# Attention and two expert layers on one core: routing columns and low parts moved from GpSimd to VectorE

## The chip, the cores and the metric

The kernel runs on one core of a Trainium2 chip. The metric is device microseconds (us) of one launch, lower is better. The core has five engines that work through instruction lists of their own in program order: TensorE (PE, with its weight loads PEld), VectorE (DVE), ScalarE (ACT), GpSimd (POOL) and SyncE (SP, which here only issues transfers). They wait for each other through semaphores.

## The reference

Chunked attention makes a matrix x of 2304 tokens by 512; a first expert layer sends each token to one of eight experts (top-1, with a capacity); a second layer weighs all eight experts with a matrix P that is normalized by rows and columns eight times.

```python
scores = scale * np.matmul(q_c, k_c.transpose(0, 1, 2, 4, 3))     # chunks of 64, B=4, H=8, S=576, D=64
attn = np.exp(scores - max); attn = attn / (attn.sum(-1) + 1e-09)
x = np.matmul(attn, v_c)                                          # then (B*S, H*D) = (2304, 512)
logits = x @ w_gate;  expert_idx = np.argmax(logits, axis=1)      # first layer, E=8, F=1024
# token i gets place counts[e] at its expert while counts[e] < capacity, and weight gate_w[i]
h = np.maximum(einsum('ecd,edf->ecf', disp, w1), 0.0);  y = einsum('ecf,efd->ecd', h, w2)
out[i] = gate_w[i] * y[expert_idx[i], pos[i]]                     # if kept
# second layer: P = exp(x @ w_gate2 - max), 8 times: rows / sum, columns / sum, * N/E
out += P[:, e:e+1] * (np.maximum(x @ w1[e], 0.0) @ w2[e])         # for all e
```

## The kernel before, in words

The kernel has three stages one behind the other: attention with routing (to about 150 us), the first expert layer (L641 to L853) and the second (L861 to L1194). The change lies in the first.

**Attention is a software pipeline written out by hand.** Its 18 tiles of 128 tokens go through 14 small steps (`st_tr` to `st_logits`). The loop at L596 runs n from 0 to 23 (called step n here), and in step n the table `order` (L593) issues each function for tile n minus its lag. So within step n an engine's instructions stand in this order: VectorE normalizes tile n-4 (`st_x1`, L390 to L393), makes the scale of tile n-5 (`st_scale`, L90 to L93), the low part of tile n-6 (`st_lo`, L416), and the row maximum and difference of tile n-2 (`st_max`, L361 and L363). ScalarE takes the exponential of tile n-3 (`st_exp`, L375), the high part of tile n-5 (`st_hi`, L412), the sum of squares of tile n-4 (`st_norm`, L401), a copy (L428), and four copies of transposed q or k (`st_tr`, L343, L346). The `manual_schedule` mode keeps that order; nothing is moved by a scheduler. GpSimd issues the store of each finished row of x (L418).

**Routing** (`route`, L442) is done for groups of three tiles. Its small VectorE steps are strewn between the pipeline's (`todo_r`): `second` of the five groups inside the loop falls on steps 9, 12, 15, 18 and 21. `r_row` (L516, VectorE) and `r_col` (L522, GpSimd) make two one-hot matrices whose product (`r_tab`, L527) fills the table `gidx` of tokens by expert and place. The sixth group comes after the loop (L626). The gathers of the first expert's tokens (L656, GpSimd) wait for `gidx` and for every store to `xs_d`, the last of which (`r_out`, L556) carries the tokens' weights.

**Expert 0's weights** are loaded and split beside this, by a plan of step numbers (L582): `w_stat` (L157, ScalarE) sums squares, `w_scale` adds them over the partitions (for expert 0 by GpSimd's `partition_all_reduce`, L176), `w_scale2` makes a power of two of it, and `w_split` makes a high and a low fp16 part of each quarter of a matrix. What is planned for step n is issued behind all else of step n. The quarters of matrix a are split at steps 10, 13, 8 and 15, those of b at 15, 14, 16 and 13, each in three instructions, VectorE, ScalarE, GpSimd (form 1):

```python
nc.vector.tensor_scalar(out=m.st[...], in0=m.st[...], scalar1=m.s, ...)          # L217
nc.scalar.copy(out=m.hi[...], in_=m.st[...])                                     # L218
nc.gpsimd.tensor_tensor(out=m.lo[...], in0=m.st[...], in1=m.hi[...], op=subtract) # L219
```

Before the loop VectorE converts the capacity (L573) and splits the second layer's gate (`gate_split`, L109), whose largest value goes through GpSimd's `partition_all_reduce` (L114).

## Time and profile before

| what | us |
|---|---|
| median of 3 runs | 1871.57 (1870.57 to 1871.91) |
| the profiled execution's own time | 1866.62 |
| its span, first to last instruction | 1864.9 |
| busy: PE / DVE / ACT / POOL | 1781.0 / 1016.5 / 721.4 / 483.1 |
| attention: GpSimd starts the first gather at | 146.32 |
| first expert layer: first matmul at | 152.87 |

The span is the part of the time in which instructions ran; 1.72 us of the profiled execution lie outside it. Busy shares over the whole span say little about the change, since it touches only the first 150 us; there the engines have to be read stretch by stretch.

### The profile page before, as it was taken

The numbers are of one execution on the slowest core, as the hardware profiler recorded it, in microseconds if no ns is written. First come the engines' busy times: TensorE is split into PE (matmuls) and PEld (weight loads), VectorE is DVE, ScalarE is ACT, GpSimd is POOL, SyncE is SP. The second block draws the span as 40 slices with busy tenths as digits, with TensorE's granted clock in tenths as the row PEclk, the third lists the DMA queues.
The fourth block names the chain that finished last, engine by engine and source line by source line (L and its number), as shares of the span: only waits on it lengthen the run. The fifth ranks groups of instructions, "written<-read, shape, count | busy, mean of one in ns | idle before, by whom it ended". The sixth has DMA issues, their size and how long they took to land.

```text
span 1864.9 us, 27396 instructions
## 1 busy us (share of the span) xinstructions
PE 1781.0 (96%) x10751; PEld 1011.4 (54%) x10751; DVE 1016.5 (55%) x1977; ACT 721.4 (39%) x1310; POOL 483.1 (26%) x498
## 2 busy tenths in 40 slices
PE   7877999888998999999999999999999999999998
PEld 5765666655454555555545555555555555555553
DVE  4896657756467734654464445355534653464432
ACT  7955556644334333441233323233322431242210
POOL 2255335541103300411031123012301321042221
PEclk9978999999999999999999999999999999999999
DMA  9746565844241203130221112112112120212200
GB/s 231 200 160 200 151 209 162 222 116 131 83 138 62 75 30 105 60 105 22 84 97 68 60 54 96 60 60 105 46 59 104 61 105 1 105 59 71 82 35 34
DMA packets 135118, 182.11 MB, mean 98 GB/s; under 512 B 62240, under 2 KB 80752, under 8 KB 134960
## 3 DMA queue, kind: packets, MB, share of 16 engines
q1 hardware_dynamic: 127968, 162.22, 28.1%
q0 software_dynamic: 5360, 17.24, 2.7%
q8 instruction: 98, 1.61, 0.4%
q14 instruction: 60, 0.49, 0.1%
q10 hardware_dynamic: 1632, 0.56, 0.1%
HBM read 149.21 MB, written 23.56 MB: 93 GB/s over the span
## 4 chain that ended last, share of the span: by engine, by line
PE 69%; DVE 4%; ACT 3%; issue 1%; POOL 1%; DMA 0%; POOLq 0%; DVEq 0%
PE p_m L1107 39%; PE p_m L1045 29%; DVE c L1051 1%; ACT eh L1061 1%; DVE el L1062 1%; ACT wsq L157 1%; POOL w L1080 1%; PE p_m L934 0%; ACT m L1070 0%; ACT m L1090 0%; PE p_l L166 0%; DVE w L222 0%; DVE u L1051 0%; ACT w L221 0%; DMA out_dram<-acc,rk 0%
## 5 line engine op out<-in xcount | busy, mean ns | idle before, releaser
L1107 PE MATMUL p_m<-w,eh 128*128 128x512 f16 x2304 | 686.2, 379 | 3.6 <-ACT eh L1061 3.6
L1045 PE MATMUL p_m<-x,w 128*128 128x384 f16 x4032 | 662.4, 326 | 1.7 <-DVE c L1051 1.3
L1045 PEld LDWEIGHTS <-w 128*128 128x128 f16 x4032 | 394.2, 98 | 263.0 <-issue 2.3
L1107 PE MATMUL p_m<-w,el 128*128 128x512 f16 x1152 | 437.1, 379 | 0.0
L1107 PEld LDWEIGHTS <-eh 128*128 128x128 f16 x2304 | 225.4, 98 | 270.7 <-ACT eh L1061 5.4
L1080 POOL TENSOR_TENSOR w<-u,m 128x384 f32<-128x384 f32 x96 | 96.6, 1006 | 970.5 <-DVE u L1051 911.3
L1061 ACT ACTIVATE eh<-c 128x384 f16<-128x384 f32 x384 | 190.3, 518 | 402.2 <-DVE c L1051 402.2
L1181 DVE SCALAR_TENSOR_TENSOR acc<-p_m,cf,acc 128x512 f32<-128x512 f32 x126 | 94.6, 750 | 383.3 <-PE p_m L1107 377.1
L1062 DVE SCALAR_TENSOR_TENSOR el<-c,eh 128x384 f16<-128x384 f32 x384 | 218.1, 569 | 126.6 <-ACT eh L1061 116.1
L1070 ACT COPY m<-p_m 128x384 f32<-128x384 f32 x96 | 44.7, 465 | 399.4 <-PE p_m L1045 399.4
L1107 PEld LDWEIGHTS <-el 128*128 128x128 f16 x1152 | 112.7, 98 | 137.1 <-DVE el L1062 1.8
L709 PEld LDWEIGHTS <-w 128*128 128x128 f16 x1152 | 106.2, 100 | 28.1 <-issue 11.2
L726 PE MATMUL p_y<-w,hh 128*128 128x512 f16 x352 | 106.6, 385 | 0.0
L709 PE MATMUL p_p<-xT,w 128*128 128x256 f16 x768 | 89.3, 278 | 9.6 <-DMA xT<-xg 3.8
L1085 POOL TENSOR_TENSOR c<-u,m 128x384 f32<-128x384 f32 x96 | 95.8, 998 | 1.5 <-DVE u L1051 1.5
L1051 DVE TENSOR_TENSOR u<-p_m,m 128x384 f32<-128x384 f32 x96 | 53.4, 556 | 59.6 <-PE p_m L1045 59.6
L1051 DVE TENSOR_TENSOR c<-p_m,w 128x384 f32<-128x384 f32 x96 | 53.5, 557 | 50.0 <-PE p_m L1045 32.2
L246 ACT ACTIVATE w<-wsum,wsa 128x1024 f16<-128x1024 f32 x32 | 36.6, 1145 | 87.1 <-POOL wsum L240 87.1
L222 DVE SCALAR_TENSOR_TENSOR w<-stb,wsb,w 128x1024 f16<-128x1024 f32 x46 | 65.3, 1431 | 6.2 <-ACT w L221 6.1
L1051 DVE TENSOR_TENSOR u<-p_m,u 128x384 f32<-128x384 f32 x96 | 53.5, 557 | 27.7 <-PE p_m L1045 25.6
L157 ACT ACTIVATE wsq<-sta 128x1024 bf16<-128x1024 f32 x64 | 67.6, 1056 | 0.9
L726 PE MATMUL p_y<-w,hl 128*128 128x512 f16 x176 | 67.7, 385 | 0.0
(232 smaller groups left out, 1664.8 us busy)
## 6 DMA issues: line engine op xcount, KB each, us to landing
x<-xt_d SPq DMA_DIRECT2D x147, 384.0 KB, 4.4
sta<-in_moe_w_dram SPq DMA_DIRECT2D x18, 1024.0 KB, 6.5
stb<-in_moe_w_dram SPq DMA_DIRECT2D x18, 1024.0 KB, 7.6
sta<-in_moe_w_dram SPq DMA_DIRECT2D x28, 512.0 KB, 8.7
stb<-in_moe_w_dram SPq DMA_DIRECT2D x28, 512.0 KB, 11.8
xt_d<-x SPq DMA_DIRECT2D x21, 384.0 KB, 3.5
x_d<-row SPq DMA_DIRECT2D x20, 256.0 KB, 4.1
vbd<-in_v_dram SPq DMA_DIRECT2D x72, 64.0 KB, 3.7
```

The lines of the kernel that those rows point to most:

```text
L157: nc.scalar.activation(out=sq, in_=src, func=AF.Square, accum_out=m.mx[:, h:h + 1])
L222: nc.vector.scalar_tensor_tensor(out=m.lo[:, sl, :], in0=m.st[:, sl, :], scalar=m.s, in1=m.hi[:, sl, :], op0=ALU.mult, op1=ALU.subtract)
L709: nc.tensor.matmul(p[:, f4, :], lhsT=w[:, kk, f * 128:(f + 1) * 128], rhs=xT[:, lo + kk, 0:W], start=(n == 0), stop=(n == 3 * KD - 1))
L726: nc.tensor.matmul(y, lhsT=h[:, kk, sl], rhs=w[:, kk, :], start=(n == 0), stop=(n == 3 * KF - 1))
L1045: nc.tensor.matmul(p, lhsT=wt[:, w, lw, kk, :], rhs=xt[:, lx, kk, :], start=(n == 0), stop=(n == 5))
L1051: nc.vector.tensor_tensor(out=c, in0=p, in1=t, op=ALU.add)
L1061: nc.scalar.activation(out=hh[:, sl], in_=src, func=AF.Relu)
L1062: nc.vector.scalar_tensor_tensor(out=hl[:, sl], in0=src, scalar=0.0, in1=hh[:, sl], op0=ALU.max, op1=ALU.subtract)
L1080: nc.gpsimd.tensor_tensor(out=Q["w"], in0=Q["u2"], in1=Q["m5"], op=ALU.add)
L1085: nc.gpsimd.tensor_tensor(out=Q["c22"], in0=Q["u3"], in1=Q["m5"], op=ALU.add)
L1107: nc.tensor.matmul(y, lhsT=h[:, t * 128:(t + 1) * 128], rhs=w[:, kk, :], start=(n == 0), stop=(n == 3 * KF - 1))
L1181: nc.vector.scalar_tensor_tensor(out=acc[:, j, :], in0=y, scalar=coefs[x][:, j:j + 1], in1=acc[:, j, :], op0=ALU.mult, op1=ALU.add)
```

## The change

It does six things. (1) `r_col` runs on VectorE. (2) The quarters of expert 0 are split in the form that the later experts use already: ScalarE makes the high part with the scale in it, and VectorE the low part (x times s, minus high) in one instruction; the last quarter of b moves from step 13 to step 17. (3) The sums over partitions of expert 0's weights are products with a matrix of ones on TensorE, and `w_scale` and `w_scale2` come a step later. (4) The capacity and the second gate are handled in steps 6 to 8, the gate's sum over partitions is a product too (a sum instead of a maximum; the exponent's offset goes from 4 to 11). (5) The sixth group's first steps and its counting product come ahead of step 23. (6) The rest of the sixth group is reordered: its weights are stored before its places are computed, and the counts come after its table.

```diff
--- before.py
+++ after.py
@@ -21,7 +21,6 @@
 EXP_MASK = 0x7F800000
-LW = 4
 LF = 10
 LM = 11
 LX = 5
@@ -107,19 +106,27 @@
     def gate_split(src, nm):
-        wgt = sm("gate", [128, KD, E])
+        wgt = const.tile([128, KD, E], F32, name="gate")
         nc.scalar.dma_start(out=wgt, in_=src.rearrange("(k p) e -> p k e", p=128))
-        gm, ga = sm("gm", [128, 1]), sm("ga", [128, 1])
-        nc.vector.tensor_reduce(out=gm, in_=wgt, axis=AX.XY, op=ALU.max, apply_absolute_value=True)
-        nc.gpsimd.partition_all_reduce(out_ap=ga, in_ap=gm, channels=128, reduce_op=bass.bass_isa.ReduceOp.max)
-        s, inv = pow2_of_max(ga, 1, LW, "gate")
         g = const.tile([128, KD, 2 * E], F16, name=nm)
-        nc.vector.tensor_scalar(out=g[:, :, 0:E], in0=wgt, scalar1=s, scalar2=None, op0=ALU.mult)
-        nc.vector.scalar_tensor_tensor(out=g[:, :, E:2 * E], in0=wgt, scalar=s, in1=g[:, :, 0:E],
-                                       op0=ALU.mult, op1=ALU.subtract)
         keep = const.tile([128, 1], F32, name=nm + "i")
-        nc.vector.tensor_copy(keep, inv)
-        return g, keep
+        t = {}
+
+        def largest():
+            t["m"] = sm("gm", [128, 1])
+            nc.vector.tensor_reduce(out=t["m"], in_=wgt, axis=AX.XY, op=ALU.max, apply_absolute_value=True)
+
+        def total():
+            t["s"] = over_partitions(t["m"], 296, 1)
+
+        def split():
+            s, inv = pow2_of_max(t["s"], 1, LM, "gate")
+            nc.vector.tensor_scalar(out=g[:, :, 0:E], in0=wgt, scalar1=s, scalar2=None, op0=ALU.mult)
+            nc.vector.scalar_tensor_tensor(out=g[:, :, E:2 * E], in0=wgt, scalar=s, in1=g[:, :, 0:E],
+                                           op0=ALU.mult, op1=ALU.subtract)
+            nc.vector.tensor_copy(keep, inv)
+
+        return g, keep, (largest, total, split)
     class Mat:
@@ -169,11 +176,7 @@
     def w_scale(x, nm):
         m = mats[x, nm]
         m.scaled = False
-        if x > 0:
-            m.am = over_partitions(m.mx, {"a": 288, "b": 292}[nm], 4)
-            return
-        m.am = smw("wam" + nm, [128, 4])
-        nc.gpsimd.partition_all_reduce(out_ap=m.am, in_ap=m.mx, channels=128, reduce_op=bass.bass_isa.ReduceOp.add)
+        m.am = over_partitions(m.mx, {"a": 288, "b": 292}[nm], 4)
     def w_scale2(x, nm):
         m = mats[x, nm]
@@ -205,17 +208,13 @@
         n = 2 * ((x - E) % 2) if x >= E else 2 * (nm == "b")
         m.hi, m.lo = (w_slot(x, n + i).rearrange("p (k n) -> p k n", n=m.n) for i in range(2))
-    def w_split(x, nm, j, nj, on_pool=0):
+    def w_split(x, nm, j, nj, on_pool=False):
         m = mats[x, nm]
         c = m.kk // nj
         sl = slice(j * c, (j + 1) * c)
-        if on_pool == 2:
+        if on_pool:
             nc.scalar.activation(out=m.hi[:, sl, :], in_=m.st[:, sl, :], func=AF.Copy, scale=m.s)
             nc.gpsimd.tensor_scalar(out=m.st[:, sl, :], in0=m.st[:, sl, :], scalar1=m.s, scalar2=None, op0=ALU.mult)
-            nc.gpsimd.tensor_tensor(out=m.lo[:, sl, :], in0=m.st[:, sl, :], in1=m.hi[:, sl, :], op=ALU.subtract)
-        elif on_pool == 1:
-            nc.vector.tensor_scalar(out=m.st[:, sl, :], in0=m.st[:, sl, :], scalar1=m.s, scalar2=None, op0=ALU.mult)
-            nc.scalar.copy(out=m.hi[:, sl, :], in_=m.st[:, sl, :])
             nc.gpsimd.tensor_tensor(out=m.lo[:, sl, :], in0=m.st[:, sl, :], in1=m.hi[:, sl, :], op=ALU.subtract)
         else:
             nc.scalar.activation(out=m.hi[:, sl, :], in_=m.st[:, sl, :], func=AF.Copy, scale=m.s)
@@ -519,7 +518,7 @@
             def r_col(j):
                 if j == 0:
                     t["cols"] = at.tile([128, G, E * NT], F16, tag="cols", name="cols")
-                nc.gpsimd.tensor_scalar(out=t["cols"][:, j, :], in0=iocf, scalar1=t["ci"][:, j:j + 1],
+                nc.vector.tensor_scalar(out=t["cols"][:, j, :], in0=iocf, scalar1=t["ci"][:, j:j + 1],
                                         scalar2=None, op0=ALU.is_equal)
             def r_tab():
@@ -570,25 +569,28 @@
             nc.gpsimd.memset(vbd[j][64:128, :, :, 129:130], 1.0)
         load_qk(1)
         nc.sync.dma_start(out=cap_i, in_=capacity.bitcast(I32).partition_broadcast(128))
-        nc.vector.tensor_copy(cap, cap_i[:, 0:1])
         nc.scalar.dma_start(out=g1, in_=w_gate.rearrange("(k p) e -> p k e", p=128))
-        g2, ig2 = gate_split(w2_gate, "g2")
+        sums["bank"] = p_tab
+        g2, ig2, g2_steps = gate_split(w2_gate, "g2")
         nc.vector.memset(ohsum[0], 0.0)
         todo = {}
         def plan(n, f):
             todo.setdefault(n, []).append(f)
-        for nm, ld, st, sc, sp in (("a", (2, 3), (3, 4, 5, 6), 6, (10, 13, 8, 15)), ("b", (9, 10), (11, 10, 12, 12), 12, (15, 14, 16, 13))):
+        plan(6, lambda: nc.vector.tensor_copy(cap, cap_i[:, 0:1]))
+        for n, f in zip((6, 7, 8), g2_steps):
+            plan(n, f)
+        for nm, ld, st, sc, sp in (("a", (2, 3), (3, 4, 5, 6), 6, (10, 13, 8, 15)), ("b", (9, 10), (11, 10, 12, 12), 12, (15, 14, 16, 17))):
             for h in range(2):
                 plan(ld[h], lambda nm=nm, h=h: w_load(0, nm, h))
                 plan(NT + 1, lambda nm=nm, h=h: w_load(1, nm, h))
             for h in range(4):
                 plan(st[h], lambda nm=nm, h=h: w_stat(0, nm, h, True))
-            plan(sc, lambda nm=nm: (w_scale(0, nm), w_alloc(0, nm)))
-            plan(sc + 1, lambda nm=nm: w_scale2(0, nm))
+            plan(sc + 1, lambda nm=nm: (w_scale(0, nm), w_alloc(0, nm)))
+            plan(sc + 2, lambda nm=nm: w_scale2(0, nm))
             for h in range(4):
-                plan(sp[h], lambda nm=nm, h=h: w_split(0, nm, h, 4, 1))
+                plan(sp[h], lambda nm=nm, h=h: w_split(0, nm, h, 4))
         order = ((st_x1, 4), (st_scale, 5), (st_exp, 3), (st_lo, 6), (st_scores, 2), (st_hi, 5), (st_norm, 4), (st_xtr, 4),
                  (st_max, 2), (st_xcopy, 4), (st_tr, 0), (st_pv, 3), (st_logits, 5), (st_dtr, 2))
@@ -599,6 +601,10 @@
             if 2 <= n < NT + 2:
                 load_v(n - 2)
             i = n - 6
+            if n == NT + 5:
+                (*first, tot1, tot2), mm, (gw, eps, rec, sel, pos, *second), tab, (kx, racc, rout) = route(NG - 1)
+                for r in first + mm:
+                    r()
             if i >= 0 and i % G == G - 1 and i < NT - G:
                 for m, part in zip((n, n + 1, n + 1, n + 3, n + 5), route(i // G)):
                     todo_r.setdefault(m, []).append(part)
@@ -623,8 +629,7 @@
             for part in todo_r[n]:
                 for r in part:
                     r()
-        (*first, tot1, tot2), mm, (gw, eps, rec, *second), tab, (kx, racc, rout) = route(NG - 1)
-        for r in first + mm + second + tab + [tot1, tot2, gw, eps, rec, racc, kx, rout]:
+        for r in [gw, eps, rec, sel, pos, kx, rout, *second, *tab, tot1, tot2, racc]:
             r()
         tot = sm("gtot", [128, 2, E, E], F16)
@@ -804,7 +809,7 @@
             if y < E:
                 for nm in "ab":
                     w_alloc(y, nm)
-                sp = [lambda h=h, nm=nm: w_split(y, nm, h, 4, 2 * (nm == "b" and h > 1)) for h, nm in
+                sp = [lambda h=h, nm=nm: w_split(y, nm, h, 4, nm == "b" and h > 1) for h, nm in
                       ((0, "a"), (2, "b"), (1, "a"), (2, "a"), (3, "b"), (3, "a"), (0, "b"), (1, "b"))]
                 sc = [lambda f=f, nm=nm: f(y, nm) for f in (w_scale, w_scale2) for nm in "ab"]
                 steps = sc + sp
```

**VectorE from the end of step 8 into step 9.** Here `sta` is the staged f32 matrix a of expert 0, `w` its fp16 part, `x1s` the scale of a tile. Before:

```order
L428 COPY xT<-p_t 128x512
L217 TENSOR_SCALAR sta_277<-sta_277,wsa 128x1024
L390 TENSOR_SCALAR rs<-p_x 128x8
L391 RECIPROCAL rs<-rs 128x8
L393 TENSOR_TENSOR x_768<-p_x,rs 128x512
L540 TENSOR_REDUCE ggw<-gex 128x3
L543 TENSOR_SCALAR ggw<-ggw 128x3
L90 TENSOR_SCALAR x1h<-ssq_696 128x1
L91 TENSOR_SCALAR x1s<-x1h 128x1
```

After the change:

```order
L187 TENSOR_REDUCE wmma<-p_tab 128x1
L89 TENSOR_SCALAR wh<-wmma 128x1
L90 TENSOR_SCALAR wsa<-wh 128x1
L92 TENSOR_SCALAR wia<-wh 128x1
L221 SCALAR_TENSOR_TENSOR w_1_630<-sta_262,wsa,w_0_629 128x1024
L389 TENSOR_SCALAR rs<-p_x 128x8
L390 RECIPROCAL rs<-rs 128x8
L392 TENSOR_TENSOR x_765<-p_x,rs 128x512
L539 TENSOR_REDUCE ggw<-gex 128x3
L542 TENSOR_SCALAR ggw<-ggw 128x3
L89 TENSOR_SCALAR x1h<-ssq_675 128x1
L90 TENSOR_SCALAR x1s<-x1h 128x1
```

The scaling of the quarter has become the subtraction that makes its low part; it reads `w`, which ScalarE writes at the end of its own step 8. The scale of the weights (L187 to L92), and ahead of that the gate's seven rows, stand before it, and step 9 with the next tile's normalization and scale stands behind it.

**VectorE before the first tile.** `gm` and `ga` are the gate's largest value by partition and over all of them. Before:

```order
L566 MEMSET kbd_157 128x2048
L573 CAST cap<-cap_i 128x1
L113 TENSOR_REDUCE gm<-gate 128x1
L79 TENSOR_SCALAR gatem<-ga 128x1
L80 TENSOR_SCALAR gatem<-gatem 128x1
L82 TENSOR_SCALAR gates<-gatem 128x1
L84 TENSOR_SCALAR gatei<-gatem 128x1
L117 TENSOR_SCALAR g_200<-gate,gates 128x4x8
L118 SCALAR_TENSOR_TENSOR g_200<-gate,gates,g_200 128x4x8
L121 COPY g2i<-gatei 128x1
L576 MEMSET ohsum_91 128x4
L361 TENSOR_REDUCE mx<-p_s 128x8
```

After the change:

```order
L565 MEMSET kbd_156 128x2048
L565 MEMSET kbd_157 128x2048
L575 MEMSET ohsum_91 128x4
L360 TENSOR_REDUCE mx<-p_s 128x8
L362 TENSOR_TENSOR d<-p_s,mx 128x512
```

The first row maximum now follows the clearing of `kbd` and of the counts.

**VectorE at the end of attention.** `gkr` is what the last store carries, `gidx` the table that the gathers read. Before, from the rows of the sixth group on:

```order
L516 TENSOR_SCALAR rows<-iorf,glo,tokf 128x128 x3
L480 TENSOR_REDUCE gohs<-goh_1982 128x8
L483 TENSOR_TENSOR ohsum_91<-ohsum_92,gohs 128x8
L540 TENSOR_REDUCE ggw<-gex 128x3
L543 TENSOR_SCALAR ggw<-ggw 128x3
L546 RECIPROCAL ggw<-ggw 128x3
L534 TENSOR_TENSOR gidx<-tacc,p_tab 128x144
L550 SCALAR_TENSOR_TENSOR gkx<-gpos,cap,ggw 128x3
L555 TENSOR_TENSOR gkr<-gkx,inv 128x24
```

After the change, from the places of the sixth group on:

```order
L491 TENSOR_REDUCE gpos<-gsel 128x3
L549 SCALAR_TENSOR_TENSOR gkx<-gpos,cap,ggw 128x3
L554 TENSOR_TENSOR gkr<-gkx,inv 128x24
L495 TENSOR_TENSOR gge<-gpos,iotf 128x54
L500 TENSOR_REDUCE ghi<-gge 128x3
L504 SCALAR_TENSOR_TENSOR glo<-ghi,gpos 128x3
L509 SCALAR_TENSOR_TENSOR gci<-gix,ghi 128x3
L515 TENSOR_SCALAR rows<-iorf,glo,tokf 128x128 x3
L521 TENSOR_SCALAR cols<-iocf,gci 128x144 x3
L479 TENSOR_REDUCE gohs<-goh_1960 128x8
L482 TENSOR_TENSOR ohsum_91<-ohsum_92,gohs 128x8
L533 TENSOR_TENSOR gidx<-tacc,p_tab 128x144
```

`gkr` now comes before L495, the three column rows (L521) stand on VectorE between the rows and the table, and the weights' sum and reciprocal (L540 to L546 before) have moved ahead of these rows. So have, ahead of the last low part, the sixth group's maximum to one-hot rows (L448 to L467 before).

## Rows read from the trace of the kernel before

**Rows 1.** Busy time by stretch: stretch, length, each engine (instructions), clock, DMA share, GB/s.

```profile
25.00:80.00 55.00, 49.09 (x536) 41.47 (x537) 41.42 (x132) 54.00 (x102) 12.96 (x16) 0.97 0.89 226
93.00:118.00 25.00, 16.07 (x148) 13.42 (x147) 24.48 (x43) 16.50 (x30) 18.67 (x14) 0.79 0.38 123
118.00:135.00 17.00, 15.41 (x164) 13.21 (x162) 16.11 (x68) 8.64 (x19) 4.80 (x8) 0.90 0.58 214
160.00:1864.90 1704.90, 1663.46 (x9600) 912.80 (x9597) 899.58 (x1619) 610.76 (x1111) 425.63 (x412) 0.99 0.28 89
```

**Rows 2.** Timeline, first tile: start us, us, engine, line, operation, what ended idle time.

```profile
11.75 1.98 PE L354 MATMUL p_s<-kbd,qT 128*64 128x128 f32 x16 [2.19 <-ACT qT L346]
16.11 0.15 DVE L79 TENSOR_SCALAR gatem<-ga 128x1 f32<-128x1 f32 x1 [4.12 <-POOL ga L114]
17.20 0.68 DVE L361 TENSOR_REDUCE mx<-p_s 128x8 f32<-128x512 f32 x1
```

**Rows 3.** Timeline and issues of SP, 16.6 to 21.8 us; TensorE's use of it.

```profile
16.63 5.19 SPq L329 DMA_DIRECT2D vbd<-in_v_dram  x4
vbd<-in_v_dram SPq DMA_DIRECT2D x4, 64.0 KB, 4.6
27.71 1.11 PE L384 MATMUL p_x<-vbd,eT 128*64 128x130 f32 x16
```

**Rows 4.** Timeline of VectorE, ScalarE and TensorE, steps 8 to 10.

```profile
51.01 0.74 DVE L217 TENSOR_SCALAR sta<-sta,wsa 128x1024 f32<-128x1024 f32 x1
51.67 0.16 DVE L390 TENSOR_SCALAR rs<-p_x 128x8 f32<-128x8 f32 x1
52.84 1.05 ACT L218 CAST w<-sta 128x1024 f16<-128x1024 f32 x1
53.16 0.15 DVE L91 TENSOR_SCALAR x1s<-x1h 128x1 int32<-128x1 int32 x1
54.41 0.71 ACT L412 ACTIVATE row<-x,x1s 128x512 f16<-128x512 f32 x1
55.00 0.86 DVE L516 TENSOR_SCALAR rows<-iorf,glo,tokf 128x128 f16<-128x128 f32 x3
56.49 0.69 DVE L363 TENSOR_TENSOR d<-p_s,mx 128x512 f32<-128x512 f32 x1
57.59 0.63 PE L370 MATMUL p_t<-ident,d 128*128 128x128 f32 x4
58.70 0.60 ACT L375 ACTIVATE eT<-p_t 128x512 f32<-128x512 f32 x1
```

**Rows 5.** Timeline of VectorE in the first expert layer: two low parts.

```profile
232.31 2.48 DVE L222 SCALAR_TENSOR_TENSOR w<-sta,wsa,w 128x1024 f16<-128x1024 f32 x2 [0.35 <-ACT w L221]
```

**Rows 6.** Timeline of VectorE at step 13 and of ScalarE at steps 14 and 15.

```profile
83.93 0.16 DVE L184 TENSOR_REDUCE wmmb<-wamb 128x1 f32<-128x4 f32 x1 [2.24 <-POOL wamb L176]
91.57 1.05 ACT L218 CAST w<-stb 128x1024 f16<-128x1024 f32 x1
93.13 0.71 ACT L412 ACTIVATE row<-x,x1s 128x512 f16<-128x512 f32 x1
```

**Rows 7.** Timeline of GpSimd and VectorE, steps 15 to 17.

```profile
93.18 2.16 POOL L219 TENSOR_TENSOR w<-sta,w 128x1024 f16<-128x1024 f32 x1 [7.66 <-ACT w L218]
93.26 2.62 DVE L416 SCALAR_TENSOR_TENSOR row<-x,x1s,row 128x512 f16<-128x512 f32 x1
113.08 1.78 DVE L458 SCALAR_TENSOR_TENSOR goh<-gd,ioef 128x24 f32<-128x24 f32 x1
```

**Rows 8.** Timeline of the end of attention.

```profile
139.43 0.18 DVE L487 TENSOR_TENSOR gsel<-goh,p_tab 128x24 f32<-128x24 f16 x1 [0.47 <-PE p_tab L476]
143.01 0.30 DVE L534 TENSOR_TENSOR gidx<-tacc,p_tab 128x144 int32<-128x144 f32 x1 [0.72 <-PE p_tab L527]
143.69 0.37 SPq L556 DMA_DIRECT2D xs_d<-gkr  x1
146.32 1.13 POOL L656 DMA_INDIRECT xg<-xs_d,gidx  x1 [3.68 <-DMA xs_d<-gkr]
```

## Prediction, made before the changed kernel ran

> **What bounds the kernel now.** I read the busy times by stretch first, then the timelines of attention, then the end of it. From 160 us on TensorE is busy 1663 of 1705 us [rows 1]; the change adds or removes nothing there, so whatever attention ends earlier or later is passed on one for one. Attention has no single bound. From 25 to 80 us ScalarE works 54.0 of 55.0 us: it is the bound, and each of its waits is lost. From 93 to 118 us VectorE works 24.48 of 25.0 us and ScalarE only 16.5. From 118 to 135 us VectorE still works 16.11 of 17.0 us [rows 1]. The reader should also see the fork that decides this case. At step 8 VectorE reaches its part of a split (L217) at 51.01 us, while ScalarE comes to its own at 52.84 us [rows 4]: before, VectorE went ahead and waited for nobody. Now its part reads what ScalarE wrote, and stands in front of all of step 9.
>
> **The head.** The first row maximum starts at 17.20 us behind the gate, which waited 4.12 us for GpSimd; its scores were done at 11.75 + 1.98 = 13.73 us [rows 2]. Without the gate it starts 0.1 us after them, at 13.85: at most 3.35 us earlier. Late next is a block of v. Its four transfers were issued until 16.63 + 5.19 = 21.82 us, with 4.6 us to landing, so about 26.4 us, and TensorE used it at 27.71 [rows 3]; that is 1.3 us of room. So the gain lies between 1.3 us, if ScalarE is soon short of that product, and 3.35, if it never is. I take 2.3, the middle, since no row is nearer to either end.
>
> **The splits.** One low part on VectorE takes 2.48 / 2 = 1.24 us [rows 5] instead of L217's 0.74 [rows 4]; ScalarE's part keeps its length within 0.1 us. Taken alone that is 8 x 0.5 = 4 us, but the wait is more. At step 8 ScalarE is done at 52.84 + 1.05 = 53.89 us. VectorE then needs 0.1 to start, 1.24 for the low part, and from L390 (51.67) to the end of L91 (53.16 + 0.15) 1.64 us for the next tile's normalization and scale. ScalarE's high part (L412) waits for that scale: it starts at 57.0 instead of 54.41 us, 2.6 us late [rows 4]. The gate's and the weights' scales at step 8 cost nothing, since VectorE would only wait longer without them.
>
> **The columns.** Three of them on VectorE are taken from L516: three rows of 128 elements took 0.86 us [rows 4], of which the next instruction overlaps about 0.1; with 144 elements that is between 0.77 and 0.97, and I take 0.81, as the setup of an instruction does not grow with its elements. In step 9, VectorE took from L91's end (53.31) to L363's end (57.18) 3.87 us; now 57.0 + 3.87 + 0.81 = 61.7, and with the 0.63 us of transposes and two hand-overs of 0.1 the exponential (L375) starts at 62.5 instead of 58.70 us [rows 4]. **Steps 8 and 9 together: +3.8.**
>
> **The other splits,** reckoned in the same way: +2.1 at step 10, where ScalarE has one more sum of squares to do while it waits; +0.8 at step 13, where VectorE already waits 2.24 us for the weights' sum [rows 6], a wait that ScalarE's part now replaces; +2.6 at step 14: ScalarE's part begins at 91.57, so the next high part begins 1.05 + 0.1 + 1.24 + 1.64 + 0.1 later, at 95.7 instead of 93.13 us [rows 6]. Four splits of one pattern, 9.3 us by the end of step 14.
>
> **What is given back.** While GpSimd subtracts (L219, 93.18 to 95.34), VectorE's L416 takes 2.62 us and ends just behind it. From it to L458 with 1.78 us [rows 7] six VectorE instructions are held so, 10.7 us together beyond what their lines take elsewhere. With GpSimd's subtractions and its columns gone these go. But at step 15 ScalarE's two parts again come last: the step is 3.1 us shorter, and step 16 begins 1.4 us sooner, together -4.5 in ScalarE's time. At steps 16 and 17 the pattern returns, with +2.3 and +2.0, the last for the split that was moved there. Then no split is left. The columns of steps 18 and 21 add 1.6, of which VectorE's 0.9 us of idle time [rows 1] takes a half to all: +0.7. **Steps 8 to 22: 3.8 + 2.1 + 0.8 + 2.6 - 4.5 + 2.3 + 2.0 + 0.7 = +9.8.**
>
> **The tail.** The gathers start at 146.32 us, 3.68 us idle behind the store of `gkr`, issued at 143.69: 2.63 us to be seen. The table's last row begins at 143.01 [rows 8]. After the change `gkr` is stored some 3.3 us earlier and is no longer last; the table is. Its chain loses the idle 0.47 and 0.72 us [rows 8], and gains 0.81 for the columns and 0.4 for the `gkr` rows ahead: it ends where it did, at 143.3, and the gathers start 0.15 later, 2.9 us earlier than before. If the columns take longer, 2.1. Expert 1's maxima stay on VectorE behind the table; I take them as hidden by the gathers, and if they are not, they cost at most the 0.4 us by which the counts now stand ahead of them. The load of expert 1's second matrix reuses the staging of the quarter that moved to step 17 and so starts later; it is needed by these maxima only, and costs nothing.
>
> **The sum.** -2.3 + 9.8 - 2.9 = **+4.6 us**. The profiled execution would go from 1866.62 to 1871.2 us; the median of the runs shown is 4.95 us above that execution, and I add the difference to the median: 1871.57 + 4.6 = 1876.2 us.
>
> **Rivals.** *VectorE is freed (faster).* If ScalarE's parts were done whenever VectorE reaches them, only VectorE's work would count: from 80 us on -10.7 (holds) - 2.2 (wait) + 6 x 0.5 + 3 x 0.81, about -7.5, with head and tail -12.7: 1858.9 us. For it speaks ScalarE's 8.5 idle us from 93 to 118 us; against it that it has one idle us from 25 to 80 [rows 1], where three of the seven split steps lie. It decides where VectorE's own step is longer than the 6 us that ScalarE needs to the end of its part. The Trainium skill stands on this side: GPSIMD Engine Reference (Engine selection) sends elementwise work to VectorE and calls GpSimd about twice as slow with two inputs. By that rule alone the eight subtractions are a plain gain; it says nothing of who waits, and the sum above goes by rows 4. The same table sends sums over partitions to GpSimd, against this change; here the row shows VectorE idle 2.24 us for one such sum, and by the rule that would have stayed, with the same result, since ScalarE's part ends later than both.
>
> *The waits shrink (no change).* ScalarE has slack behind 93 us. If it is ahead at steps 16 and 17, their 4.3 us go and the sum is +0.3: 1871.9 us. Against it: its high part at each of these steps still waits for VectorE's scale.
>
> *TensorE's clock falls (slower still).* From 93 to 118 us the granted clock is 0.79 on average, with TensorE busy 16 of 25 us [rows 1], against 0.97 at 49 of 55. If the new waits bring it to that for steps 8 to 17, each step's transposes and products on the path, about 2 us, grow by a quarter: 8 x 0.5, or +8.6 in all: 1880.2 us.
>
> **Chances.** The sum as forecast 0.44, the falling clock 0.13, the shrinking waits 0.27, VectorE freed 0.16. The likeliest case alone spans the bounds of head, columns and tail and a half us at four waits: +2 to +7, 1873.6 to 1878.6. The range of 1867.0 to 1881.0 takes in the two neighbours and the near side of the freed case, leaving out about 0.2. A measurement here tells about 0.2%, 3.7 us, from no change; of the forecast's 0.44 some 0.10 lie below that. So slower 0.34 + 0.13 = 0.47, same 0.10 + 0.27 = 0.37, faster 0.16.
>
> **What would show it.** Right: VectorE idle before its low parts (L221 in the new numbering) at steps 8, 10, 13, 14, 16 and 17, "behind ScalarE's w", with 1 to 5 us each; ScalarE idle about 2 to 3 us before the next high part; no held instruction of 1.5 us or more; the first row maximum near 13.9 us; GpSimd's first gather near 150.9 us with the table as its releaser. Wrong: if the low parts show no idle time ahead of them, or the first gather comes before 147 us; then the waits were not there and the time falls. If the first gather comes after 155 us, the columns or the clock cost more than I took.

## The result, and the profile after

The changed kernel is **slower**: 1885.63 us median of 4 runs (1883.96 to 1887.87) beside 1871.07 for the kernel before (4 runs, 1870.20 to 1871.91), a ratio of 1.0064 with a 95% interval of 1.0048 to 1.008. The forecast was 1876.2 us, in a range that ended at 1881.0: the direction was right and the loss some three times too small. The profiled execution took 1887.87 us, with a span of 1886.0.

Three marks carry what follows: the end of attention (the last low part of a row on VectorE), the first gather, and the first product of the first expert. From before to after they go from 137.56 to 150.45 us (+12.9), from 146.32 to 156.67 (+10.4), and from 152.87 to 163.19 (+10.3). From there to the end it is 1712.0 us before and 1722.8 after: another +10.8 us that the change should not have touched. The two profiled executions lie 21.3 us apart, the medians 14.6: the one before is 4.5 us below its median, the one after 2.2 above, so differences between these two traces come out somewhat large.

Busy time by stretch of the changed kernel (columns as in rows 1):

```profile
25.00:80.00 55.00, 46.84 (x483) 40.16 (x483) 38.02 (x132) 44.43 (x82) 4.04 (x7) 0.91 0.80 203
93.00:118.00 25.00, 21.99 (x178) 19.18 (x176) 17.84 (x53) 18.20 (x30) 2.41 (x4) 0.70 0.20 59
118.00:135.00 17.00, 12.02 (x110) 10.17 (x110) 14.10 (x53) 9.03 (x17) 1.24 (x3) 0.81 0.84 281
160.00:1886.00 1726.00, 1673.47 (x9670) 921.74 (x9670) 900.27 (x1633) 614.06 (x1115) 428.23 (x418) 0.99 0.28 89
```

Where one engine was full before [rows 1], none is now: from 25 to 80 us ScalarE works 44.4 of 55 us in place of 54.0, from 93 to 118 us VectorE 17.8 of 25 in place of 24.5 (part of that is the held time that is gone). Where neither is full, time goes into waiting for each other. The step 8 of rows 4 shows how, in the timeline of ScalarE and VectorE:

```profile
51.25 1.15 ACT L220 ACTIVATE w<-sta,wsa 128x1024 f16<-128x1024 f32 x1
52.43 1.28 DVE L221 SCALAR_TENSOR_TENSOR w<-sta,wsa,w 128x1024 f16<-128x1024 f32 x1 [1.33 <-ACT w L220]
55.13 0.15 DVE L90 TENSOR_SCALAR x1s<-x1h 128x1 int32<-128x1 int32 x1
55.32 0.72 ACT L411 ACTIVATE row<-x,x1s 128x512 f16<-128x512 f32 x1 [2.30 <-DVE x1s L90]
```

VectorE waits 1.33 us for ScalarE's high part, does its low part and step 9's normalization, and only then makes the scale that ScalarE has been waiting for, 2.30 us. The view of waits from 43 to 130 us counts them:

```profile
DVE w L221 <- ACT w L220: 19.2, 7, 5.1
ACT row L411 <- DVE x1s L90: 7.7, 4, 2.3
ACT gex L453 <- DVE gd L451: 7.6, 3, 2.9
```

Seven waits of VectorE ahead of low parts, 19.2 us, up to 5.1 us; and ScalarE waits back, 7.7 us for the scales and 7.6 us for the routing's difference (`gd`), whose exponential stands in front of the attention's; before, these two were 1.3 and 3.0 us. No VectorE instruction of 1.5 us or more is left from step 8 to the end of attention (the holds behind GpSimd's subtractions [rows 7] are gone).

The head and the tail of attention (answering to rows 2, 3 and 8):

```profile
13.22 0.69 DVE L360 TENSOR_REDUCE mx<-p_s 128x8 f32<-128x512 f32 x1 [6.31 <-PE p_s L353]
26.10 2.72 PE L383 MATMUL p_x<-vbd,eT 128*64 128x130 f32 x16 [3.19 <-DMA vbd<-in_v_dram]
154.74 0.30 DVE L533 TENSOR_TENSOR gidx<-tacc,p_tab 128x144 int32<-128x144 f32 x1
155.56 0.17 PE L641 MATMUL p_tab<-gohx,ones 128*128 128x16 f16 x1 [0.85 <-DVE gohx L640]
156.67 1.05 POOL L661 DMA_INDIRECT xg<-xs_d,gidx  x1 [4.57 <-PE p_tab L641]
```

The first maximum comes 4.0 us earlier, and most of that is given back at once to a block of v that TensorE has to wait for. In the tail, the store of `gkr` is no longer last, but the gathers don't follow the table directly either: their wait ends with the product of the counts (L641, done at 155.73 us, 0.7 us behind the table), and the first of them starts 0.9 us later.

The rest is in the experts, which the change leaves alone. In the last but one of them (timelines of SyncE and TensorE) the kernel before shows

```profile
376.48 5.23 SPq L146 DMA_DIRECT2D stb<-in_moe_w_dram  x4
377.04 2.73 PE L709 MATMUL p_p<-xTc,w 128*128 128x128 f16 x46
381.90 2.95 PE L709 MATMUL p_p<-xTc,w 128*128 128x128 f16 x50 [2.13 <-issue]
```

and the changed kernel

```profile
389.83 1.98 SPq L153 DMA_DIRECT2D stb<-in_moe_w_dram  x4
390.91 2.39 PE L714 MATMUL p_p<-xTc,w 128*128 128x128 f16 x40
398.67 4.68 PE L714 MATMUL p_p<-xTc,w 128*128 128x128 f16 x56 [5.37 <-issue]
```

TensorE breaks off in the middle of a block of 96 products, waiting for nothing that the profile shows ("issue"): 2.13 us before, 5.37 after.

### The profile page after: what moved, and what is told of

It reads as the page before. It is cut to its first block, busy times and chain, and to the rows that moved or that the text cites. A ratio compares the mean times of both kernels' runs of the same rounds, so it can differ in the third digit from the quotient of the medians.

```text
span 1886.0 us, 27385 instructions
## 1 busy us (share of the span) xinstructions
PE 1790.6 (95%) x10757; PEld 1021.3 (54%) x10757; DVE 1009.2 (54%) x1995; ACT 722.6 (38%) x1310; POOL 450.6 (24%) x469
## 4 chain that ended last, share of the span: by engine, by line
PE 68%; DVE 4%; ACT 3%; issue 1%; POOL 1%; DMA 0%; POOLq 0%; DVEq 0%
PE p_m L1112 39%; PE p_m L1050 28%; DVE c L1056 1%; ACT eh L1066 1%; DVE el L1067 1%; ACT wsq L164 1%; POOL w L1085 1%; PE p_m L939 0%; ACT m L1075 0%; ACT m L1095 0%; PE p_l L173 0%; DVE w L221 0%; DVE u L1056 0%; ACT w L220 0%; DMA out_dram<-acc,rk 0%
## 5 line engine op out<-in xcount | busy, mean ns | idle before, releaser
L221 DVE SCALAR_TENSOR_TENSOR w<-stb,wsb,w 128x1024 f16<-128x1024 f32 x50 | 66.1, 1334 | 13.0 <-ACT w L220 12.9
```

What stands on the lines that cost most here:

```text
L221: nc.vector.scalar_tensor_tensor(out=m.lo[:, sl, :], in0=m.st[:, sl, :], scalar=m.s, in1=m.hi[:, sl, :], op0=ALU.mult, op1=ALU.subtract)
```

## The experiments

Two theories about attention: **the waits** (VectorE stands behind ScalarE's high part, and ScalarE then behind VectorE) against **the work** (eight low parts of 1.28 us and the columns are too much for VectorE, wherever they stand). Two more on what is left: **TensorE's clock**, and **the load** in front of the block above. Ratios are to runs of the kernel before on the same chip.

| kernel | first expert product at, us | from it to the next stage's first product, us | median, us | ratio (95%) |
|---|---|---|---|---|
| before | 152.87 | 272.3 | 1868.8 to 1871.5 | 1 |
| changed | 163.19 | 282.7 | 1885.63 | 1.0064 (1.0048 to 1.008) |
| changed, again | 160.29 | 280.0 | 1884.57 | 1.0066 (1.004 to 1.0092) |
| changed, old form of split | 152.56 | 273.7 | 1872.10 | 1.0013 (0.9996 to 1.0029) |
| changed, step 17's quarter at 14 | 159.83 | 276.7 | 1877.59 | 1.0034 (1.0016 to 1.0051) |
| changed, columns on GpSimd | 161.37 | 275.2 | 1880.26 | 1.0048 (1.0031 to 1.0065) |
| before, new form of split alone | 163.86 | 272.6 | 1881.73 | 1.0057 (1.0035 to 1.0079) |
| changed, low parts a step late | 144.85 | 275.7 | 1865.61 | 0.9977 (0.9962 to 0.9992) |
| the same, columns on GpSimd | 143.80 | 281.8 | 1861.95 | 0.9956 (0.9941 to 0.9971) |
| before, new form, low parts late | 149.17 | 270.3 | 1864.65 | 0.9988 (0.9975 to 1.0001) |
| late, two low parts behind the tail | 155.60 | 277.3 | 1874.26 | 1.0021 (1.0008 to 1.0035) |
| changed, products as filling (table's bank) | 170.57 | 275.3 | 1891.61 | 1.012 (1.0092 to 1.0149) |
| changed, products as filling (logits' bank) | 165.97 | 287.5 | 1893.30 | 1.0132 (1.0117 to 1.0148) |
| changed, load moved | 162.73 | 276.7 | 1880.64 | 1.0049 (1.0031 to 1.0067) |
| late, columns on GpSimd, load moved | 142.08 | 277.6 | 1859.03 | **0.9928** (0.9912 to 0.9945) |

**The form of the splits undone.**

```diff
+        elif x == 0:
+            nc.vector.tensor_scalar(out=m.st[...], in0=m.st[...], scalar1=m.s, ...)
+            nc.scalar.copy(out=m.hi[...], in_=m.st[...])
+            nc.gpsimd.tensor_tensor(out=m.lo[...], in0=m.st[...], in1=m.hi[...], op=ALU.subtract)
```

> The changed kernel, with expert 0's eight splits back in the old form (VectorE scales, ScalarE casts, GpSimd subtracts); all else as changed, the last quarter at step 17 too. In the changed kernel the first expert product (TensorE, L714) starts at 163.19 us, before at 152.87. Theory of the waits: VectorE's waits ahead of the low parts are the loss; without them the first expert product comes near 150 to 153 us and the time falls by 10 to 13 us, to about 1873 to 1876 (1869 to 1872 if what was lost behind the first gather goes too). Rival, the columns and the clock alone: the product stays at 158 us or later and the time falls by less than 5 us.

Hit at the mark: 152.56 us, 10.6 earlier (by the ratios the time falls by 9.5 us). The other five parts of the change together are worth nothing beside the old form: 0.3 us at this mark, a ratio of 1.0013. The price of the old form is still there, five held instructions on VectorE, of which the longest is

```profile
94.17 2.64 DVE L419 SCALAR_TENSOR_TENSOR row<-x,x1s,row 128x512 f16<-128x512 f32 x1
```

**The form alone**, on the kernel before.

```diff
-                plan(sp[h], lambda nm=nm, h=h: w_split(0, nm, h, 4, 1))
+                plan(sp[h], lambda nm=nm, h=h: w_split(0, nm, h, 4))
```

> The kernel before with nothing changed but the form of expert 0's eight splits (ScalarE's scaled copy, then VectorE's low part, in the same step; the last quarter stays at step 13). Theory of the waits: the form alone is the loss; the first expert product comes at 158 to 163 us in place of 152.87, with VectorE idle 1 to 5 us ahead of the low parts. Rival, VectorE freed from GpSimd's holds: at 152 us or earlier.

163.86 us, 0.9 beyond the range on the side of the waits; VectorE freed is refuted. The row of the waits is the changed kernel's over again:

```profile
DVE w L222 <- ACT w L221: 19.5, 7, 5.4
```

**The low parts a step late.**

```diff
-                plan(sp[h], lambda nm=nm, h=h: w_split(0, nm, h, 4))
+                plan(sp[h], lambda nm=nm, h=h: w_split(0, nm, h, 4, part="hi"))
+                plan(sp[h] + 1, lambda nm=nm, h=h: w_split(0, nm, h, 4, part="lo"))
```

> The changed kernel, with each low part of expert 0's splits issued one step later than its high part, at the end of the next step. The work on each engine is the same. Theory of the waits: VectorE finds the high part done and waits for nothing; the first expert product comes near 150 to 153 us and the time falls by 10 to 13 us. Rival, VectorE's added work (eight parts of 1.28 us) is the loss, wherever it stands: the product stays within 3 us of 163.2 and the time within 3 us of the changed kernel's.

144.85 us: 18.3 earlier than the changed kernel (15.4 earlier than its second profile, below), 8.0 earlier than before, more than I expected. The work is the same to the instruction; only the step of eight of them differs. All waits of VectorE that are left from 43 to 130 us:

```profile
DVE rs L391 <- PE p_x L385: 5.4, 3, 2.0
DVE mx L362 <- PE p_s L355: 0.5, 2, 0.2
```

None is for ScalarE. ScalarE still waits 6.0 us for the scales; what went are VectorE's 19.2 us. In kind that is the rival "VectorE is freed" of the forecast; but it took the order of eight instructions to get there, and the change didn't have it.

**The same on the kernel before**, with no other edit.

> The kernel before with nothing changed but the splits: the new form, and each low part one step after its high part (columns on GpSimd, gate and tail as before). Theory, the step in which the low part stands decides, and the rest of the change is worth 1 to 5 us: the first expert product comes at 145 to 149 us (152.87 before, 143.80 with all the rest and the columns on GpSimd), the time 4 to 8 us below before. Rival, late low parts pay only with the other edits: 152 us or later.

149.17 us, just past the far end of the range, and 3.7 us before the kernel before; by medians 5.2 us below it, by the ratio less, with an interval that reaches 1. The late low part pays at the mark without the other edits, if less; in the time that is not clear of no change. The rest with the columns on GpSimd is then worth 149.17 - 143.80 = 5.4 us; while the waits stood in front of it, it was 163.86 - 161.37 = 2.5 us (the changed kernel with its columns on GpSimd, next).

**The columns back on GpSimd**, in the changed kernel and in the one with late low parts.

```diff
-                nc.vector.tensor_scalar(out=t["cols"][:, j, :], in0=iocf, ...
+                nc.gpsimd.tensor_scalar(out=t["cols"][:, j, :], in0=iocf, ...
```

> The changed kernel, with the columns (r_col) back on GpSimd; all else as changed. By my sum the columns cost 0.8 us at step 9 and 0.7 at steps 18 and 21, and the tail 0.8: the first expert product comes 1 to 2.5 us earlier and the time falls by as much. Rival, the columns as the main loss: 5 us or more. Rival on the other side: GpSimd's columns hold VectorE as before and delay the table, and the time rises by 1 to 3 us.

> The kernel with the low parts one step late, and the columns back on GpSimd, which has nothing else to do there. VectorE worked 24.2 of 25 us from 93 to 118 in the kernel with late low parts (first expert product at 144.85 us). Theory, VectorE is the bound there: 3 x 0.61 us per third step less brings the first expert product to 141 to 144 us. Rival, VectorE's instructions are held while GpSimd makes columns, and the last table comes later: 145 to 147 us.

1.8 us and 1.05 us earlier, both inside what I expected and both small. The first can't be told from the 2.9 us by which two profiles of the changed kernel differ (next). Nor can the second: the last kernel of the table is the same up to the experts, and its mark is at 142.08 us, another 1.7 earlier.

**The changed kernel again.**

> The changed kernel, unchanged, beside more runs of the kernel before. From first look to last row, attention and tail explain +10.3 us of its time (the first expert product at 163.19 in place of 152.87 us); the rest of its +14.6 us stood behind that, at 350 to 425 us. Theory, that rest differs from run to run: the first expert product comes at 163.2 us again within 0.5, the ratio is 1.0045 to 1.0065. Rival, the change slows the experts' stage itself by 4 us: 1.0075 or more.

The ratio came back (1.0066), the first expert product did not: 160.29 us. The instructions are the same; busy time and clock from 93 to 104 and from 128 to 139 us are not. The first profile, then the second:

```profile
93.00:104.00 11.00, 11.00 (x74) 9.93 (x73) 9.06 (x36) 7.84 (x15) 1.09 (x2) 0.50 0.17 50
128.00:139.00 11.00, 10.28 (x70) 8.35 (x70) 8.45 (x33) 4.21 (x9) 1.87 (x3) 0.53 0.68 240
```

```profile
93.00:104.00 11.00, 8.18 (x85) 7.20 (x83) 9.00 (x35) 8.58 (x16) 1.09 (x2) 0.84 0.22 70
128.00:139.00 11.00, 9.42 (x79) 7.93 (x79) 9.65 (x37) 4.30 (x11) 1.87 (x3) 0.71 0.57 213
```

With TensorE at 1.2 GHz throughout the first stretch (0.50), it is busy all 11 us with 74 products; in the second profile it does 85 in 8.2 us. The kernel with the load moved (below) has the changed kernel's attention too, and so is a third profile of it: low clock again, and the first expert product at 162.73 us.

```profile
93.00:104.00 11.00, 11.00 (x73) 9.59 (x72) 9.05 (x36) 7.84 (x15) 1.09 (x2) 0.50 0.21 66
128.00:139.00 11.00, 10.35 (x71) 8.59 (x71) 8.41 (x29) 4.03 (x9) 1.86 (x3) 0.54 0.66 237
```

So the clock goes with up to 2.9 us of the loss in attention.

**The clock, by filling TensorE's gaps.** Two tries, eight more products a step whose result nobody reads.

```diff
+                if f is st_scores and n in (13, 15, 16, 18, 19):
+                    for _ in range(8):
+                        nc.tensor.matmul(p_g[:, 256:384], lhsT=ident, rhs=ident)
```

> The changed kernel with eight more TensorE products (128x128, of the identity, into unused columns of the table's bank) behind the scores of steps 14 to 19, where TensorE waited for VectorE. The added products' result is not used. Theory of the clock: TensorE stays at 2.4 GHz from 128 to 139 us (granted clock 0.9 or more, in place of 0.53), and the first expert product comes 3 to 4.5 us earlier, 158.7 to 160.2. Rival, the clock is not on the path: no earlier than 162.5, or up to 2 us later for the added products.

> The changed kernel with eight more TensorE products (of the identity, into unused columns of the logits' bank, their result not used) behind the scores of steps 13, 15, 16, 18 and 19, with no wait of their own. In two profiles of the changed kernel the clock differed (0.50 and 0.84 from 93 to 104 us, 0.53 and 0.71 from 128 to 139) and the first expert product came at 163.19 and 160.29. Theory of the clock: it stays at 0.9 or more in both stretches, and the product comes at 157 to 159.5 us, before the better of the two. Rival, the clock is not on the path, and VectorE's waits alone set the time: 160 to 163 us at whatever clock.

Both missed. In the first (into the table's bank, steps 13 to 19) the clock rose, to 0.90 and 0.86 in the two stretches, but the added products themselves waited for VectorE's last reading of that bank:

```profile
135.04 2.91 PE L625 MATMUL p_tab<-ident 128*128 128x128 f32 x16 [3.17 <-DVE gsel L486]
```

In the second the clock was 0.54 and 0.84, and the first expert product came at 165.97 us; the added products' own time stands in that, so this try does not price the clock either. That the clock causes those 2.9 us is therefore argued from the three profiles, not shown.

**The quarter of step 17 at step 14.**

```diff
-(11, 10, 12, 12), 12, (15, 14, 16, 17))
+(11, 10, 12, 12), 12, (15, 14, 16, 14))
```

> The changed kernel, with one split moved: the last quarter of b at step 14 in place of step 17. Theory of the clock: TensorE ran at 1.2 GHz from 127.8 to 138.7 us behind the wait of step 17, and that cost about 3.6 us beyond the wait itself; without that wait the first expert product comes 4 to 5.5 us earlier (157.7 to 159.2) and TensorE is at 2.4 GHz in the last four steps. Theory of the waits alone: a second split at step 14 waits 1 to 2 us there and the 2 us of step 17 go, so 0 to 1 us earlier.

3.4 us earlier than the first profile of the changed kernel, 0.5 earlier than the second: inconclusive.

**Two low parts behind the tail.**

```diff
-                plan(sp[h] + 1, ... part="lo"))
+                if sp[h] < 16:
+                    plan(sp[h] + 1, ... part="lo"))
...
         nc.vector.tensor_copy(reg_i[:, 0:2 * E], p_tab[:, 256:256 + 2 * E])
+        for h in (2, 3):
+            w_split(0, "b", h, 4, part="lo")
```

> The kernel with late low parts and columns on GpSimd, and the last two low parts moved behind the tail, where VectorE waits for the gathers; expert 1's maxima of its second matrix stand behind the first transposes' copies. VectorE is the bound of the last steps, so two parts of 1.2 us less there bring the first expert product from 143.80 to 141 to 142 us, and the time falls by 1.5 to 2.5 us more. Rival, the second half of expert 1's second matrix is loaded later (its staging is free later), the maxima wait for it, and TensorE loses 2 us or more in the first expert: no gain or a loss in time.

A miss by a mechanism I had not listed. The low parts keep expert 1's load (L153) waiting for its staging, and SyncE issues in order: behind that load stand the last three stores of rows, which SyncE issues itself and without which no gather starts. Issued behind the load, stores also took some 9 us to land; the last one, of `gkr`, took 1.7 us in the kernel before. The timeline of SyncE, then the issues with KB each and us to landing:

```profile
136.15 0.92 SPq L153 DMA_DIRECT2D stb<-in_moe_w_dram  x2
137.16 1.73 SPq L419 DMA_DIRECT2D xs_d<-row  x3
xs_d<-row SPq DMA_DIRECT2D x3, 256.0 KB, 9.2
xs_d<-gkr SPq DMA_DIRECT2D x1, 12.0 KB, 9.0
```

Attention's last row on VectorE came 2.8 us earlier than with all low parts in the loop (1.0 earlier than in the other profile of that attention), the first gather 11.7 us later.

**The load in the experts.** In five profiles (the changed kernel's two, step 14, late with columns on GpSimd, two behind the tail) the first of the four loads was issued 0.64 to 1.08 us ahead of the block (two or three of them in all, the rest behind its start), and the break in it took 4.2 to 5.4 us. In the others without filling the lead was 0.56 us or less, or the loads came behind the start, and the break took 0 to 2.1 us. A lead alone does not make a break: in the like block of the first expert, loads are issued 1.35 us ahead in every kernel, and none breaks there; and one of the kernels with filling had a lead of 1.11 us and a break of 2.48.

```diff
-                if x == E - 2:
-                    loads(E, "b")
...
-            sites += [behind, []]
+            sites += [behind, [lambda: loads(E, "b")] if x == E - 2 else []]
```

> The changed kernel with one load moved: the four 512 KB loads for the next stage, issued by SyncE in the last but one expert just ahead of a block of TensorE products, come a row later. In both profiles of the changed kernel they were issued 0.8 to 1.1 us ahead of that block, and TensorE then stood 5.4 and 5.1 us in the middle of it waiting for nothing the profile shows (issue). Theory, its instructions are fetched behind those 2 MB: the wait shrinks to 2.2 us or less, and from the first expert product to the first product of the next stage it takes 273 to 277 us in place of 282.7 and 280.0. Rival, the stretch differs for other reasons: the wait stays at 4 us or more, or the stretch at 279 us or more.

```profile
389.05 2.39 PE L714 MATMUL p_p<-xTc,w 128*128 128x128 f16 x40
393.54 4.91 PE L714 MATMUL p_p<-xTc,w 128*128 128x128 f16 x56 [2.10 <-issue]
393.74 2.69 SPq L153 DMA_DIRECT2D stb<-in_moe_w_dram  x4
```

> The kernel with late low parts and columns on GpSimd, with the same load moved. There the wait was 5.0 us and the stretch 281.8 us; the time was 0.9956 of before. Theory: wait 2.2 us or less, stretch 274 to 277, the time 0.993 of before or less. Rival: no shorter wait, ratio 0.995 to 0.997.

```profile
370.83 2.39 PE L717 MATMUL p_p<-xTc,w 128*128 128x128 f16 x40
375.21 3.29 PE L717 MATMUL p_p<-xTc,w 128*128 128x128 f16 x56 [1.99 <-issue]
375.58 6.13 SPq L153 DMA_DIRECT2D stb<-in_moe_w_dram  x4
```

Hit for the break: 2.10 and 1.99 us. The stretches are 276.7 and 277.6 us (3.3 to 6.0 and 4.2 us shorter; the second 0.6 over what I expected), and only some 3 us of that is the break. The rest lies in other waits of TensorE, one of them ahead of the moved load: for gathered tokens it waited 2.78 and 3.84 us in the changed kernel's profiles at 370 to 380 us, and 1.02 in this one. In the time, the intervals of the ratios with and without the move still overlap in both pairs. The last kernel, late low parts, columns on GpSimd and the load moved, **beats both**: 1859.03 us, 0.7% below before.

## Why the prediction was wrong

**Right in kind: the splits.** The mechanism, the place and the sign were as forecast; step 8's wait of ScalarE is 2.30 us beside the 2.6 worked out, and by the exponential of step 10 [rows 4] the loss of steps 8 and 9 is 3.5 us (58.70 to 60.70, from 1.5 ahead to 2.0 behind) beside 3.8. From the exponential of step 9 to that of step 18 the changed kernel loses 8.1 us in one profile and 5.6 in the other (from 1.5 and 0.6 ahead to 6.6 and 5.0 behind), beside the 7.1 that the sum has for steps 8 to 16: the sizes bracket it.

**Too small: the last steps.** From the exponential of step 18 to the last row's low part it took 18.7 us before, 25.0 and 23.7 after: +6.3 and +5.0, for which "+2.0 for step 17" and "+0.7 for columns" stood in the sum. Three pieces can be told apart by the exponentials that follow. From step 18 to step 19 it is +3.0 in all three profiles of this attention (before, then after):

```profile
118.84 0.60 ACT L375 ACTIVATE eT<-p_t 128x512 f32<-128x512 f32 x1 [1.26 <-PE p_t L370]
124.35 0.60 ACT L375 ACTIVATE eT<-p_t 128x512 f32<-128x512 f32 x1 [2.10 <-PE p_t L370]
125.43 0.60 ACT L374 ACTIVATE eT<-p_t 128x512 f32<-128x512 f32 x1
133.98 0.60 ACT L374 ACTIVATE eT<-p_t 128x512 f32<-128x512 f32 x1 [3.85 <-PE p_t L369]
```

With the quarter of step 17 at step 14 these 3.0 are 1.2, with the columns on GpSimd 2.4: about 1.9 and 0.6, close to the two terms. From step 19 to step 20 it is another +2.0, +0.7 and +2.0, the 0.7 in the profile whose clock from 128 to 139 us was 0.71 and not 0.53 or 0.54. The clock was given no term in the sum; the rival "TensorE's clock falls" put 4.0 us on all split steps together, and how much it cost is not shown. The last +1.3, from there to the last low part, is the same in the kernel with the old form of split, so it has nothing to do with the splits; the sixth group's rows that moved ahead of that low part are the likely reason.

**Nearly right: head and tail, the tail by luck.** The head gave 1.5 us in one profile and 0.6 in the other (the exponential of step 9 at 52.42 and 53.31 in place of 53.92), around its lower bound of 1.3, for the reason named there: the block of v. I took the middle between two bounds although the row of v's transfers [rows 3] already said which one holds. The tail gave 12.9 - 10.4 = 2.5 us beside 2.9, but not as worked out. From the last low part to the end of the table it took 5.75 us before and 4.59 after, 1.2 less where I had no gain, about what the +1.3 above had moved ahead of it; and from the table to the first gather it took 1.6 us where I had 0.15: the product of the counts, which I had overlooked, came last, and the gather started 0.9 us behind it. Of the checks named, the first maximum (13.22 beside 13.9), the waits of 1 to 5 us, ScalarE's 2 to 3 us and the missing holds came as forecast; the first gather came at 156.67, past the 155 us that was to mean that the columns or the clock cost more, and its releaser was not the table.

**The step that failed: "whatever attention ends earlier or later is passed on one for one".** Attention and tail make +7.4 to +10.3 us where the sum has 4.6; the whole is +14.4 to +14.6 by medians. The rest, 4 to 7 us by medians, is the experts, for which the sum has nothing. In the traces their stretch takes 280.0 and 282.7 us in place of 272.3 (more than the medians leave for it, as the traced execution of the kernel before was below its median). Of these 7.7 and 10.4 us the break in the one block makes 3.0 and 3.2. The others are waits spread over the stretch, such as this one for gathered tokens, which the trace of before does not have, and the last one for SyncE (after twice, then before):

```profile
379.53 0.68 PE L679 MATMUL p_t<-id,xg 128*128 128x128 f16 x9 [2.78 <-DMA xg<-xs_d,gidx]
445.90 1.68 PE L939 MATMUL p_m<-id,head 128*128 128x128 f16 x14 [8.06 <-SPq L846]
425.12 1.67 PE L934 MATMUL p_m<-id,head 128*128 128x128 f16 x14 [6.07 <-SPq L841]
```

With the load moved the break is back to 2.1 us, and the stretch is still 4.4 us longer than in the trace of before. What causes that part stays open; the form of split alone, on the kernel before, lost its 11.0 us in attention and nothing in the experts (272.6 us). I had read from rows 1 that TensorE is busy there 1663 of 1705 us and that the change adds nothing to it; both hold. But a stretch that is full by its average still has waits inside it, and for one of them, the break, two runs show that it changes with the moment at which a load is issued; the change had shifted that moment against TensorE's work. Why the load comes ahead in some kernels and behind in others was not settled.

## What to carry to other kernels

When an elementwise step moves from an engine that nobody waits for to one that everybody waits for, its own duration (here 1.28 us) says little; what its operand waits for, and what is queued behind it, says the rest. Here the same eight instructions, with nothing else changed, cost 11.0 us at the first expert product in the step of their producer, and gave 3.7 us when they stood one step later (8.0 with the rest of the change). Before you move work off a tightly wound loop, look also at what is issued behind it on each DMA queue: here a load whose buffer came free late held every store behind it, 11.7 us at the first gather.

## What was not expected of the hardware

TensorE's break in the block, where there is one, stands at the same product, the 40th of 96 in kernels made from the changed one and the 46th in those made from the one before, whenever the block begins (the two kernels with filling apart; the kernel before with the new form alone has no break), and there is no semaphore to wait for. That speaks for a fetch of instructions. DMA queues of the kind "instruction" carry packets there (the changed kernel, 385 to 405 us; packets, MB, share of 16 engines):

```profile
q8 instruction: 3, 0.05, 1.0%
q14 instruction: 2, 0.02, 0.2%
```

But they carry the same packets and bytes around this block in the kernel that has no break there (before with the new form alone, 384 to 404 us), so these rows alone decide nothing. The break takes up to 2.1 us, and 4.2 to 5.4 where the first of the loads was issued at least 0.64 us ahead of the block. The Trainium skill (Runtime: NRT & Kernel Launch, Instruction fetch mechanics) says that each engine's sequencer fetches its instructions by a DMA queue of its own, that crossing a block's boundary is "mostly hidden", and that a taken branch can break the prefetch; this block stands behind a branch. The two kernels with the load moved agree with a fetch by DMA; if it is one, "mostly hidden" doesn't hold here. That it is a fetch is inferred from this, not seen, and the blocks with loads ahead of them and no break speak for a further condition that no run here shows.

In two profiles of the same kernel, TensorE ran a stretch of 11 us at 1.2 GHz throughout in the one (granted clock 0.50) and mostly at 2.4 in the other (0.84), with the end of attention 2.9 us apart. A single profile of a stretch with gaps is no measure of a change of that size.
